# A fused attention and feed-forward kernel: a planned issue order, DMA transposes of q, k and x, and one score burst per block

## The chip, the cores and the metric

The kernel runs on one core of a Trainium2 chip. The metric is the device time of one execution in microseconds (us); lower is better. Executions carry a state, fast or slow.

PE is TensorE's matmuls and PEld its weight loads. DVE is VectorE, ACT is ScalarE, POOL is GpSimd. SP is the engine that issues most DMAs; "SPq" in a profile line is time in which SP's sequencer is occupied by issuing one.

## The reference

For each batch and head, scores are masked to a local window of 96 positions and 8 global positions, with a linear distance bias. The result of attention goes through a two-layer network with softplus:

```python
# q, k, v: (4, 8, 768, 64), float32; n_global 8, n_local 96
scores = q @ k.T / sqrt(64) - slope[h] * dist     # -1e9 where neither local nor global
a = softmax(scores)
x = (a @ v)                # regrouped as (3072 tokens, 512)
h = x @ w_in               # w_in (512, 2048)
g = softplus(h)            # log(1 + exp(h))
out = g @ w_out            # w_out (2048, 512), out (3072, 512) float32
```

## The kernel before

Tokens go in 24 blocks of 128; two blocks make a window of 256. Attention of later windows is interleaved with the two layers of earlier ones, by a hand-made list of event times. Within a window, partition p holds tokens 2p and 2p+1, so that a q or k load reads runs of 512 bytes.

q and k are cast to bf16, transposed by TensorE and copied out of PSUM; x is treated likewise. Scores are computed in two half bursts a block, four heads each, and DVE adds the bias.

```python
def load(w):
    nc.sync.dma_start(q32[:], q[b, :, sl, :].rearrange("h (p r) d -> p h (r d)", r=2))
    # k the same; v in four pieces of 256-byte runs
    ...
def transp(w, which, psum, eng):
    for r in range(2):
        for m in range(NPAIR):                  # 8 matmuls for a window of q or of k
            nc.tensor.transpose(tr[:, m, r, :], src[...], ident[:])
    cast_on[eng](t[:], psum...)                 # PSUM to SBUF
...
def scores(n, half, psum):
    for lh in range(4):
        nc.tensor.matmul(psum[:, reg_base(lh), :], kt_of(n)[rows, m, :], qT[rows, m, :])
        if i > 0:
            nc.tensor.matmul(psum[:, reg_base(lh) + 1, :], kt_of(n - 1)[rows, m, :], qT[rows, m, :])
    ...                                         # DVE: z = scores + bias
def mm2(g, p):                                  # second layer: two output banks
    for ns in range(2):
        for j in range(2):
            nc.tensor.matmul(o_ps[ns][:], gt[...], w_out_bf[...], ...)
```

The softmax here doesn't subtract the row's maximum and nothing guards it: scores larger than these inputs give would overflow.

Of the kernel before, what the change touches and what calls it, by code (L numbers as in the profile page):

```python
# [1 line left out]

# [8 lines left out]
ALU = mybir.AluOpType  # L11
F32 = mybir.dt.float32
BF16 = mybir.dt.bfloat16


@with_exitstack
def kernel(
# [33 lines left out]
    NGRP = NT // W  # L51
    NS = 4
    GH = NG // 2

    slopes = [2.0 ** (-8.0 * (h + 1) / H) for h in range(H)]

    root_d = float(D) ** 0.5
    perm = [0, 2, 1, 3]

    def reg_base(lh):  # L60
        return 4 * (lh % 2) + 2 * (lh // 2)

    ctx.enter_context(tc.manual_schedule())

    const = ctx.enter_context(tc.tile_pool(name="const", bufs=1))
    raw = ctx.enter_context(tc.tile_pool(name="raw", bufs=3))
    qkv = ctx.enter_context(tc.tile_pool(name="qkv", bufs=2))
    ring = ctx.enter_context(tc.tile_pool(name="ring", bufs=5))
    work = ctx.enter_context(tc.tile_pool(name="work", bufs=3))
    ffn = ctx.enter_context(tc.tile_pool(name="ffn", bufs=3))  # L70
    ps = ctx.enter_context(tc.tile_pool(name="ps", bufs=1, space=bass.MemoryType.PSUM))

    s_ps = ps.tile([P, 8, P], F32, name="s_ps")
    x_ps = ps.tile([P, 512], F32, name="x_ps")
    tr_ps = ps.tile([P, 1024], BF16, name="tr_ps")

# [9 lines left out]


    state = {}

    def load(w):  # L90
        b, ww = divmod(w, WPB)
        sl = slice(W * ww, W * ww + W)
        q32 = raw.tile([P, H, 2 * D], F32, tag="q32", name="q32")
        nc.sync.dma_start(q32[:], q[b, :, sl, :].rearrange("h (p r) d -> p h (r d)", r=2))
        k32 = raw.tile([P, H, 2 * D], F32, tag="k32", name="k32")
        nc.sync.dma_start(k32[:], k[b, :, sl, :].rearrange("h (p r) d -> p h (r d)", r=2))
        v32 = raw.tile([P, 2, H, D], F32, tag="v32", name="v32")
        for blk in range(2):
            t0 = W * ww + P * blk
            vv = v[b, :, t0 : t0 + P, :].rearrange("h (p r) d -> r p h d", r=2)  # L100
            for r in range(2):
                nc.sync.dma_start(v32[64 * r : 64 * r + 64, blk, :, :], vv[r])  # L102
        state["raw", w] = (q32, k32, v32)

    cast_on = {"pool": nc.gpsimd.tensor_copy, "dve": nc.vector.tensor_copy, "act": nc.scalar.copy}

    def cast(w, which, eng):
        q32, k32, v32 = state["raw", w]
        copy = cast_on[eng]
        if which in "qk":  # L110
            src = q32 if which == "q" else k32
            t = qkv.tile([P, 2, H, D], BF16, tag=which + "b", name=which + "b")
            copy(t[:], src[:].rearrange("p h (r d) -> p r h d", r=2))  # L113
            state[which + "b", w] = t
        else:
            t = ring.tile([P, 2, H, D + 1], BF16, tag="vb", name="vb")
            copy(t[:, :, :, 0:D], v32[:])
            nc.gpsimd.memset(t[:, :, :, D : D + 1], 1.0)
            state["vb", w] = t

    def transp(w, which, psum, eng):
        src = state[which + "b", w]
        tr = psum.rearrange("p (m r t) -> p m r t", m=NPAIR, r=2)
        for r in range(2):
            for m in range(NPAIR):
                nc.tensor.transpose(  # L126
                    tr[:, m, r, :],
                    src[:, r, 2 * m : 2 * m + 2, :].rearrange("p a b -> p (a b)"),
                    ident[:],
                )  # L130
        t = (ring if which == "k" else qkv).tile(
            [P, 2, NPAIR * 2, 64], BF16, tag=which + "T", name=which + "T"
        )
        cast_on[eng](t[:], psum.rearrange("p (a b t) -> p b a t", b=2, t=64))  # L134
        state[which + "T", w] = t

    def kt_of(n):
        return state["kT", n // 2][:, n % 2, :, :].rearrange("p (m r) t -> p m (r t)", r=2)

    def vb_of(n):  # L140
        return state["vb", n // 2][:, n % 2, :, :]

    def globals_k(n):


        first = n - n % NBLK
        kd = state["kT", (n - 1) // 2][:, (n - 1) % 2, :, 0:GH]
        nc.gpsimd.tensor_copy(kd, state["kT", first // 2][:, 0, :, 0:GH])  # L148

    def globals_v(n):  # L150
        first = n - n % NBLK
        for r in range(2):
            sl = slice(64 * r, 64 * r + GH)
            nc.vector.tensor_copy(vb_of(n - 1)[sl, :, 0:D], vb_of(first)[sl, :, 0:D])  # L154

    def scores(n, half, psum):
        i = n % NBLK
        qT = state["qT", n // 2][:, n % 2, :, :].rearrange("p (m r) t -> p m (r t)", r=2)
        for lh in range(4):
            h = 4 * half + lh  # L160
            m, sub = h // 2, h % 2
            rows = slice(64 * sub, 64 * sub + 64)
            nc.tensor.matmul(psum[:, reg_base(lh), :], kt_of(n)[rows, m, :], qT[rows, m, :])  # L163
            if i > 0:
                nc.tensor.matmul(  # L165
                    psum[:, reg_base(lh) + 1, :], kt_of(n - 1)[rows, m, :], qT[rows, m, :]
                )
        z = work.tile([P, 8, P], F32, tag="z", name="z")
        if i == 0:
            nc.vector.tensor_tensor(z[:, 0:4, :], psum[:, 0:8:2, :], bias0[:, half, :, :], ALU.add)  # L170
        else:
            nc.vector.tensor_tensor(z[:], psum[:, :, :], biasA[:, half, :, :], ALU.add)  # L172
        state["z", n, half] = z

    def expo(n, half):
        nr = 4 if n % NBLK == 0 else 8
        z = state.pop(("z", n, half))
        pb = work.tile([P, 8, P], BF16, tag="pb", name="pb")
        nc.scalar.activation(pb[:, 0:nr, :], z[:, 0:nr, :], AF.Exp, scale=1.0 / root_d)  # L179
        state["pb", n, half] = pb  # L180

    def pv(n, half, psum):
        i = n % NBLK
        pb = state.pop(("pb", n, half))
        if half == 0:
            state["xs", n] = work.tile([P, H, D], BF16, tag="xs", name="xs")
        xs = state["xs", n]
        xv = psum[:, 0 : 4 * (D + 1)].rearrange("p (h e) -> p h e", e=D + 1)
        for lh in range(4):
            h = 4 * half + lh  # L190
            j = perm.index(lh)
            if i == 0:
                nc.tensor.matmul(xv[:, lh, :], pb[:, j, :], vb_of(n)[:, h, :])
            else:
                nc.tensor.matmul(  # L195
                    xv[:, lh, :], pb[:, 2 * j, :], vb_of(n)[:, h, :], start=True, stop=False
                )
                nc.tensor.matmul(  # L198
                    xv[:, lh, :], pb[:, 2 * j + 1, :], vb_of(n - 1)[:, h, :], start=False, stop=True
                )  # L200
        rcp = work.tile([P, 4], F32, tag="rcp", name="rcp")
        nc.vector.reciprocal(rcp[:], xv[:, :, D : D + 1].rearrange("p h e -> p (h e)"))  # L202
        nc.vector.tensor_tensor(  # L203
            xs[:, 4 * half : 4 * half + 4, :],
            xv[:, :, 0:D],
            rcp[:][:, :, None].to_broadcast([P, 4, D]),
            ALU.mult,
        )

    def x_transp(n, psum, eng):  # L210
        xs = state.pop(("xs", n))
        tr = psum[:, 0:512].rearrange("p (m t) -> p m t", m=NPAIR)
        for m in range(NPAIR):
            nc.tensor.transpose(  # L214
                tr[:, m, :], xs[:, 2 * m : 2 * m + 2, :].rearrange("p a b -> p (a b)"), ident[:]
            )
        cast_on[eng](XT[:, :, P * n : P * n + P], tr)  # L217

    def mm1(g, p):
        hv = h_ps[state["hslot"]][:].rearrange("p (j t) -> p j t", j=2)  # L220
        state["hslot"] ^= 1
        for j in range(2):
            fb = 2 * p + j
            for m in range(NM):
                nc.tensor.matmul(  # L225
                    hv[:, j, :],
                    w_in_bf[:, m, fb * P : fb * P + P],
                    XT[:, m, W * g : W * g + W],
                    start=(m == 0),
                    stop=(m == NM - 1),  # L230
                )
        if p % 2 == 0:
            state["e", g] = ffn.tile([P, 2, 512], F32, tag="e", name="e")
        if p == 0:
            state["g", g] = ffn.tile([P, NFB, W], BF16, tag="g", name="g")
        e = state["e", g]
        nc.scalar.activation(e[:, p % 2, :].rearrange("p (j t) -> p j t", j=2), hv, AF.Exp)  # L237
        if p % 2 == 1:
# [4 lines left out]
                bias=1.0,  # L243
            )

    def mm2(g, p):
        gt = state["g", g]
        for ns in range(2):
            for j in range(2):
# [216 lines left out]
```

## Time and profile before

| | before |
|---|---|
| time, median of 2 runs | 259.94 us |
| span of the profiled run | 256.0 us |
| PE busy | 225.1 us, 88% |
| first-layer matmuls started by 52 us | 51 of 768 |
| second-layer matmuls started by 52 us | 12 of 384 |

The first lines to read are those of the page that cut the span into 40 slices. Each digit is the busy share of a slice in tenths; the DMA row is the mean busy share of the core's 16 DMA engines.

```profile
span 256.0 us, 5170 instructions
...
PE   1437687399999999999999999999999999999991
...
DMA  7999999999965095192291590300202003003033
```

PE is starved for the first eight slices while DMA is full; then PE is full to the end. The table by stretches says it in microseconds (columns: stretch, length, busy time and count of PE, PEld, DVE, ACT and POOL, granted PE clock, DMA share, GB/s; the DMA share adds up the times of packets, which can overlap, so it can pass 1):

```profile
0.00:52.00 52.00, 27.28 (x247) 18.76 (x248) 26.62 (x63) 21.78 (x26) 15.04 (x29) 0.94 1.17 224
52.00:88.00 36.00, 35.66 (x367) 25.36 (x366) 22.04 (x42) 26.59 (x37) 6.65 (x11) 0.99 0.76 160
88.00:196.00 108.00, 108.00 (x1090) 75.43 (x1089) 68.78 (x134) 74.85 (x98) 12.79 (x25) 1.00 0.40 89
```

PE is busy for all of 88 to 196. Its waits after 52 us (what waited, on whom; us in total, times, longest) are next to nothing:

```profile
PE o_ps_349 L251 <- DVE osb L260: 0.4, 1, 0.4
PE o_ps_349 L251 <- ACT g L239: 0.3, 1, 0.3
```

The start is bound by DMA. The chain of waits there (start, us, what) is a v load that takes 17 us while five windows and the weights share the queues:

```profile
28.38 2.02 SPq L102
...
30.44 17.32 DMA v_338<-in_v_dram
```

What one group of matmuls costs is read from starts, not from durations, because matmuls overlap. From PE's timeline, in a stretch where it never waits:

```profile
126.33 0.61 PE L126 MATMUL tr_ps<-ident,qb 128*128 128x128 bf16 x8
126.78 0.29 PE L193 MATMUL x_ps<-vb,pb 128*128 128x65 bf16 x4
```

The eight transposes of q occupy PE for 126.78 - 126.33 = 0.45 us, 0.056 us each. Read in this way, a window cost PE about 17.9 us.

### The profile page before, as it was taken

Reading aid. Unit: us, or ns where it says so; the run is one execution under the profiler, and the core shown is the slowest. Engines: PE = TensorE matmul, PEld = TensorE weight load, DVE = VectorE, ACT = ScalarE, POOL = GpSimd, SP = SyncE. Lnnn points to the kernel's source line nnn. Section 1 sums busy time; section 2 is a strip of 40 time slices with the busy share of each in tenths; the row PEclk is TensorE's granted clock in tenths of the full one; section 3 lists DMA queues with packets and bytes.
Section 4 is the critical chain, followed back from the end, with each engine's and each line's share of the span. In section 5 each row is a group of like instructions: output and inputs, shape, how many; then the busy total and the mean of one; then the engine's idle time right before and its main releaser. Section 6 shows DMA issues by size and latency. Waiting matters only on the chain.

```text
span 256.0 us, 5170 instructions
## 1 busy us (share of the span) xinstructions
PE 225.1 (88%) x2144; PEld 154.6 (60%) x2144; DVE 139.1 (54%) x279; ACT 156.2 (61%) x201; POOL 34.9 (14%) x66
## 2 busy tenths in 40 slices
PE   1437687399999999999999999999999999999991
PEld 1324465177667677666776766676676667666640
DVE  6475832246674865764665757746656757430012
ACT  2455544087876767767665777766577677766600
POOL 2142810130300300303001103030000000000000
PEclk9999999689999999999999999999999999999998
DMA  7999999999965095192291590300202003003033
GB/s 188 250 250 199 257 197 199 245 233 240 178 177 105 5 244 86 41 242 48 64 240 30 127 203 0 85 0 22 63 3 65 20 1 86 0 3 82 0 82 82
DMA packets 58391, 29.69 MB, mean 116 GB/s; under 512 B 26624, under 2 KB 55296, under 8 KB 58368
## 3 DMA queue, kind: packets, MB, share of 16 engines
q1 hardware_dynamic: 54144, 25.17, 45.5%
q0 software_dynamic: 4224, 4.19, 9.7%
q8 instruction: 16, 0.26, 0.5%
q14 instruction: 7, 0.06, 0.1%
HBM read 27.26 MB, written 6.29 MB: 131 GB/s over the span
## 4 chain that ended last, share of the span: by engine, by line
PE 79%; DMA 9%; ACT 3%; SPq 3%; DVE 3%; issue 1%; DVEq 0%; POOL 0%; POOLq 0%
PE o_ps_349 L251 17%; PE h_ps_348 L225 16%; PE o_ps_350 L251 16%; PE h_ps_347 L225 15%; DMA v_338<-in_v_dram 7%; PE s_ps L163 4%; PE tr_ps L126 3%; SPq L102 2%; DMA k_84<-in_k_dram 2%; PE tr_ps L214 2%; PE s_ps L165 2%; PE x_ps L195 2%; PE x_ps L198 2%; DVE z L172 1%; ACT g L239 1%
## 5 line engine op out<-in xcount | busy, mean ns | idle before, releaser
L225 PEld LDWEIGHTS <-w_in_bf 128*128 128x128 bf16 x768 | 73.2, 99 | 22.0 <-DVE XT L217 0.7
L172 DVE TENSOR_TENSOR z<-s_ps,biasA 128x1024 f32<-128x1024 f32 x38 | 46.4, 1220 | 26.1 <-PE s_ps L165 26.0
L251 PE MATMUL o_ps_349<-w_out_bf,g 128*128 128x512 bf16 x192 | 57.7, 383 | 1.1 <-ACT g L239 0.7
L251 PE MATMUL o_ps_350<-w_out_bf,g 128*128 128x512 bf16 x192 | 57.6, 382 | 0.0
L179 ACT ACTIVATE pb<-z 128x1024 bf16<-128x1024 f32 (+1 forms) x48 | 46.8, 975 | 14.4 <-DVE z L172 13.2
L237 ACT ACTIVATE e<-h_ps_348 128x512 f32<-128x512 f32 x48 | 28.6, 596 | 40.8 <-PE h_ps_348 L225 40.8
L251 PEld LDWEIGHTS <-g 128*128 128x128 bf16 x384 | 35.1, 98 | 29.8 <-issue 1.7
L225 PE MATMUL h_ps_347<-XT,w_in_bf 128*128 128x256 bf16 x384 | 51.5, 279 | 0.5 <-DVE XT L217 0.5
L239 ACT ACTIVATE g<-e 128x1024 bf16<-128x1024 f32 x48 | 50.7, 1057 | 1.5
L225 PE MATMUL h_ps_348<-XT,w_in_bf 128*128 128x256 bf16 x384 | 50.8, 276 | 0.0
L237 ACT ACTIVATE e<-h_ps_347 128x512 f32<-128x512 f32 x48 | 28.3, 589 | 22.2 <-PE h_ps_347 L225 22.0
L260 DVE COPY osb<-o_ps_349 128x512 f32<-128x512 f32 x12 | 8.3, 692 | 24.1 <-PE o_ps_349 L251 23.6
L202 DVE RECIPROCAL rcp<-x_ps 128x4 f32<-128x4 f32 x46 | 8.1, 176 | 24.4 <-PE x_ps L198 24.4
L203 DVE TENSOR_TENSOR xs<-x_ps,rcp 128x256 bf16<-128x256 f32 x46 | 19.5, 425 | 1.6
L148 POOL COPY kT<-kT 128x32 bf16<-128x32 bf16 x16 | 3.4, 213 | 121.0 <-PE s_ps L165 116.4
L126 PE MATMUL tr_ps<-ident,qb 128*128 128x128 bf16 x96 | 8.6, 242 | 11.7 <-DVE qb L113 11.7
L163 PE MATMUL s_ps<-qT,kT 64*128 64x128 bf16 x180 | 16.2, 231 | 2.8 <-ACT kT L134 2.2
L165 PE MATMUL s_ps<-qT,kT 64*128 64x128 bf16 x152 | 13.8, 228 | 5.5 <-POOL kT L148 5.5
L195 PE MATMUL x_ps<-vb,pb 128*128 128x65 bf16 x156 | 15.5, 198 | 1.3 <-DVE xs L203 1.3
L163 PEld LDWEIGHTS <-kT 64*128 64x128 bf16 x192 | 8.6, 99 | 12.3 <-issue 8.2
L198 PE MATMUL x_ps<-vb,pb 128*128 128x65 bf16 x156 | 15.4, 198 | 0.6 <-DVE vb L154 0.6
L134 DVE COPY qT<-tr_ps 128x1024 bf16<-128x1024 bf16 x11 | 7.6, 692 | 13.3 <-PE tr_ps L126 13.2
(86 smaller groups left out, 181.0 us busy)
## 6 DMA issues: line engine op xcount, KB each, us to landing
out_dram<-osb SPq DMA_DIRECT2D x48, 128.0 KB, 2.4
w_in_bf<-in_moe_w_in_dram POOLq DMA_DIRECT2D x4, 512.0 KB, 11.9
w_out_bf<-in_moe_w_out_dram POOLq DMA_DIRECT2D x4, 512.0 KB, 14.6
q_82<-in_q_dram SPq DMA_DIRECT2D x1, 512.0 KB, 4.2
k_84<-in_k_dram SPq DMA_DIRECT2D x1, 512.0 KB, 6.1
v_86<-in_v_dram SPq DMA_DIRECT2D x4, 128.0 KB, 5.0
q_91<-in_q_dram SPq DMA_DIRECT2D x1, 512.0 KB, 5.5
k_93<-in_k_dram SPq DMA_DIRECT2D x1, 512.0 KB, 7.0
```

The costliest lines, as they stand in the source:

```text
L126: nc.tensor.transpose(tr[:, m, r, :], src[:, r, 2 * m : 2 * m + 2, :].rearrange("p a b -> p (a b)"), ident[:],)
L163: nc.tensor.matmul(psum[:, reg_base(lh), :], kt_of(n)[rows, m, :], qT[rows, m, :])
L165: nc.tensor.matmul(psum[:, reg_base(lh) + 1, :], kt_of(n - 1)[rows, m, :], qT[rows, m, :])
L172: nc.vector.tensor_tensor(z[:], psum[:, :, :], biasA[:, half, :, :], ALU.add)
L179: nc.scalar.activation(pb[:, 0:nr, :], z[:, 0:nr, :], AF.Exp, scale=1.0 / root_d)
L195: nc.tensor.matmul(xv[:, lh, :], pb[:, 2 * j, :], vb_of(n)[:, h, :], start=True, stop=False)
L198: nc.tensor.matmul(xv[:, lh, :], pb[:, 2 * j + 1, :], vb_of(n - 1)[:, h, :], start=False, stop=True)
L203: nc.vector.tensor_tensor(xs[:, 4 * half : 4 * half + 4, :], xv[:, :, 0:D], rcp[:][:, :, None].to_broadcast([P, 4, D]), ALU.mult,)
L225: nc.tensor.matmul(hv[:, j, :], w_in_bf[:, m, fb * P : fb * P + P], XT[:, m, W * g : W * g + W], start=(m == 0), stop=(m == NM - 1),)
L237: nc.scalar.activation(e[:, p % 2, :].rearrange("p (j t) -> p j t", j=2), hv, AF.Exp)
L239: nc.scalar.activation(state["g", g][:, 2 * p - 2 : 2 * p + 2, :].rearrange("p a t -> p (a t)"), e[:].rearrange("p a t -> p (a t)"), AF.Ln ...
L251: nc.tensor.matmul(o_ps[ns][:], gt[:, fb, ns * P : ns * P + P], w_out_bf[:, fb, :], start=(fb == 0), stop=(fb == NFB - 1),)
```

## The change

The intent is to take transposes off the full engine and to fill the start. A small planner now simulates the engines with assumed durations and emits each engine's instructions in the simulated order. q and k from window 3 on, and x from block 4 on, are transposed by DMAs issued from SP. A block's 16 score matmuls are one burst over four PSUM banks; for that, one output bank and the bank of the transposes are given up. In the first four blocks TensorE adds a bf16 bias by a matmul with the identity. v is loaded in 512-byte runs, and the early loads and weights have an order of their own.

The diff is long; this is its core, with cuts marked.

```diff
+class Planner:      # list scheduling by rank over assumed durations; engines and DMA queues
+    LAT = {"PE": 0.30, "DVE": 0.12, "ACT": 0.12, "POOL": 0.15, "SP": 0.0}
 ...
-    for r in range(2):
-        for m in range(NPAIR):
-            nc.tensor.transpose(tr[:, m, r, :], ...)
+    if key is None:                       # q, k of windows 3 to 11
+        def fn():
+            for r in range(2):
+                for blk in range(2):
+                    last = nc.sync.dma_start_transpose(
+                        dst[:, blk, :, 64 * r : 64 * r + 64],
+                        src[64 * blk : 64 * blk + 64, r, :, :].rearrange("p h d -> p (h d)"))
+            return last
+        op(f"tr{which}{w}", "SP", 1.2, rank, fn, ..., dma=(1.6, 40.0))
 ...
+    # x of blocks 4 to 23
+    nc.sync.dma_start_transpose(XT[:, :, cols], xs[:].rearrange("p h d -> p (h d)"))
+    op(f"xt{n}", "SP", 0.42, rank, fn, ..., dma=(0.8, 40.0))
 ...
+    for m in range(NPAIR):                # one burst a block, row groups alternate
+        for u in range(u_all):
+            for part in range(2):
+                rows = slice(64 * part, 64 * part + 64)
+                nc.tensor.matmul(s_ps[:, reg, :], kt_of(n - u)[rows, m, :], qTt[rows, m, :], ...)
 ...
+    if biased:                            # blocks 0 to 3
+        nc.tensor.matmul(bank(key), ident[:], src[:, 512 * j : 512 * j + 512], start=True, stop=False)
 ...
-    o_ps = [late.tile([P, 512], F32, name=f"o_ps{i}") for i in range(2)]
+    o_ps = ps.tile([P, 512], F32, name="o_ps")
```

The numbers after "SP" are durations that the planner assumes: 1.2 us for the four transposes of a q or k window and 0.42 us for one of x.

## The prediction

> **What bounds the kernel now.** TensorE from 52 us on. The page gives PE 225.1 us busy of a 256.0 us span; the table by stretches shows PE busy 36.00 of 36.00 us in each stretch from 88 to 196, and PE's waits after 52 us sum to 0.7 us. Before 52 us it is starved (27 us busy, DMA share about 1.0 and over). There the chain of waits runs through one v load (17.3 us) and its issue (6.4 us), because five windows and all weights share the queues; only 54 of 768 first-layer matmuls are done by 52 us. The tail after the last matmul is 5.8 us.
>
> **One window (256 tokens) on PE**, from issue pitches in the timeline at 115 to 135 us: first layer 8 x 0.87 us and second layer 32 x 0.217, together 13.9; q and k transposes 16 x 0.056 = 0.9; x transposes 2 x 0.23 = 0.46; scores four half bursts of 0.33 plus 0.1 of gap, 1.7; probabilities times v 4 x 0.24 = 0.96. Sum 17.9, which matches the chain's repeat of 9.0 us per block.
>
> **What the change does.** It takes q and k transposes off PE from window 3, x transposes from block 4, and halves the number of score bursts (estimate from the pitch: 0.68 us a burst, so 0.3 saved a window). Together 1.65 us a window, 15 us over nine windows. It adds 14 bias matmuls of 0.22 us (3 us). PE's pure work, estimated: FFN 166.6, scores 15.6, values 10.6, remaining transposes 4, bias 3: 200 us (before 211).
> The start changes more: v comes in 512-byte runs instead of 256, w_in slices are queued early, three windows ahead of them. I expect first-layer matmuls from 16 us and, by 45 to 50 us, that layer of two to three groups done. PE's lost time at the start falls from about 35 us (52 less 17 of useful issue) to 13. DVE (139 us) and ACT (156 us) don't bound, but ACT will be near 75% busy.
>
> **Sum**: 200 + 13 lost at the start + 5.5 tail + 5 of new PE stalls (one output bank instead of two; orders planned with assumed durations) = 223.5 span; the time lies 3.9 above the span now, so **227 us**, range 219 to 239. Faster by over 2%: 0.95; within 2%: 0.03; slower: 0.02.
>
> **The open point** is the DMA transpose, in no trace yet. The Trainium skill, "VectorE: DVE Perf Modes", The three transpose paths, lists 1309 ns for a 128x128 tile by DMA; 24 tiles a window in series would be 31 us, above the 16.2 us window. "DMA: Bandwidth & Descriptors", Latency and other measured facts, gives 261 GB/s, by which I estimate 3 us for 0.79 MB. I side with the second: 16 engines share it, and attention runs over a window ahead.
>
> **Signs.** Right: PE over 90% busy from 30 us on; about 224 fewer transposes on PE; first-layer matmuls before 20 us; SP's queue busy below 70% of a window; ten DMA transposes a window landing in under 6 us. Wrong: PE waiting for kT, qT or XT from DMA once per window; over 1 us of SP issue per transpose; PE waiting over 0.5 us for each output copy.
>
> **What would break it**: transposes that fill SP's queue or hold the loads behind them; a late DMA under a fixed order, stalling PE in every window; weights landing after 55 us.

## The result, and the profile after

The changed kernel took 276.36 us (two runs, 275.71 and 277.01) against 259.94 us. The ratio is 1.065, 95% interval 1.056 to 1.073: slower. Ratios here and below are the mean time of one kernel's fast runs over that of the other's in the same rounds, so they are not quite the ratio of the medians quoted.

```profile
span 275.2 us, 4814 instructions
...
PE   2759777949249977598789968959974999999973
...
DMA  4899999593244656628767556648267372200111
```

PE now has holes everywhere. By stretches:

```profile
0.00:52.00 52.00, 37.14 (x347) 26.15 (x351) 24.19 (x69) 27.52 (x35) 21.89 (x44) 1.00 1.02 206
52.00:88.00 36.00, 23.17 (x219) 13.91 (x220) 17.23 (x33) 10.74 (x14) 7.60 (x15) 0.86 0.49 119
88.00:196.00 108.00, 91.21 (x825) 62.79 (x836) 49.93 (x90) 70.60 (x91) 23.36 (x42) 0.94 0.61 142
```

The start did improve: by 52 us, 128 first-layer matmuls have been started, against 51. The gain is lost at once: 13 us of the next 36 are idle, and 17 of the 108 after that. Idle PE also loses clock, 0.86 and 0.94 instead of 0.99 and 1.00. The Trainium skill ("TensorE: Matmul & The Clock Gate", Part 1) describes this as a gate that slows the array after idle stretches; the trace agrees: PE's longest wait, 8.6 us, ends at 79.3 us, and from 75.8 to 82.6 us the granted clock is 0.50. The clock shown for the first 52 us says less: the trace has no record of it before 24.6 us and counts it as full, though the first transposes start 107 ns apart, twice the 56 ns read above.

PE's waits, longest first in total:

```profile
PE x_ps L535 <- DVE xs L548: 9.0, 3, 3.8
PE h_ps L593 <- DMA XT<-xs: 8.6, 1, 8.6
PE s_ps L485 <- DMA kT<-kb: 8.3, 5, 3.2
PE o_ps L635 <- DVE osb L652: 6.4, 5, 2.2
PE s_ps L467 <- DVE bias L723: 5.2, 1, 5.2
```

They name different tiles, so the list alone gives no cause. SP's queue does. Its instructions in part of a window (start, us occupied, what, count):

```profile
89.42 0.39 SPq L293 DMA_DIRECT2D k<-in_k_dram  x1
89.90 1.87 SPq L578 DMA_TRANSPOSE XT<-xs  x1
91.90 5.47 SPq L369 DMA_TRANSPOSE qT<-qb  x4
97.48 0.52 SPq L293 DMA_DIRECT2D v<-in_v_dram  x1
98.10 1.21 SPq L578 DMA_TRANSPOSE XT<-xs  x1
99.41 5.07 SPq L369 DMA_TRANSPOSE kT<-kb  x4
104.57 0.53 SPq L293 DMA_DIRECT2D q<-in_q_dram  x1
```

A plain load occupies SP for about 0.5 us, a transpose for 1.2. The view by tile gives minimum, median and maximum in ns over all of them:

```profile
L369 SPq DMA_TRANSPOSE qT<-qb x36: 1171/1240/2665, 45.8 to 216.1; - x36
L578 SPq DMA_TRANSPOSE XT<-xs x20: 1189/1210/2516, 62.9 to 235.6; - x20
```

Eight of 1.24 and two of 1.21 are 12.3 us a window; three loads of about 0.5 and two stores of about 0.5 bring it to about 15 us, nearly all of the 16.2 us that I had counted for a window on PE. Between 88 and 196 us SP is occupied for 82 us of 108, 70 of them by transposes (each instruction's own time in the trace, summed). It is not quite full, but it works in order, so a load whose buffer is free still stands behind transposes, and a transpose waits for its cast. The chain of waits shows both:

```profile
99.41 1.19 SPq L369
100.65 1.24 SPq L369
101.94 2.38 DMA kT<-kb
105.81 7.14 DMA k<-in_k_dram
114.94 1.07 PE h_ps L593 x5
```

The k transposes are issued one by one, the scores of the window's first block wait for the third of the four (the last that they need) to land, and the next k load leaves at 105.81, behind all four. DVE's order is fixed too, so its cast of that k stands before the work that would free PE:

```profile
113.04 0.69 DVE L320 CAST kb<-k 128x1024 bf16<-128x1024 f32 x1 [1.70 <-DMA v<-in_v_dram]
113.65 0.18 DVE L547 RECIPROCAL rcp<-x_ps 128x4 f32<-128x4 f32 x1
113.86 0.42 DVE L548 TENSOR_TENSOR xs<-x_ps,rcp 128x256 bf16<-128x256 f32 x1
```

PE continues at 114.34, right after the last of these. That is how a late load reads as "PE waits for DVE xs".

### The profile page after: what moved, and what is told of

The parts are those of the page before. It is cut to its first block, busy times and chain, and to the rows that moved or that the text cites. A ratio compares the mean times of both kernels' runs of the same rounds, so it can differ in the third digit from the quotient of the medians.

```text
span 275.2 us, 4814 instructions
## 1 busy us (share of the span) xinstructions
PE 218.3 (79%) x1905; PEld 146.2 (53%) x1934; DVE 113.1 (41%) x227; ACT 152.4 (55%) x193; POOL 62.0 (23%) x117
## 4 chain that ended last, share of the span: by engine, by line
PE 46%; DMA 22%; SPq 14%; DVE 9%; issue 5%; ACT 2%; DVEq 0%
PE o_ps L635 20%; PE h_ps L593 18%; DMA q<-in_q_dram 11%; SPq L369 9%; DMA kT<-kb 6%; DMA k<-in_k_dram 4%; PE s_ps L485 3%; SPq L298 3%; DVE z L510 3%; DVE osb L652 2%; DVE xs L548 2%; PE x_ps L535 1%; PE x_ps L538 1%; SPq L578 1%; ACT e L609 1%
## 5 line engine op out<-in xcount | busy, mean ns | idle before, releaser
L593 PE MATMUL h_ps<-XT,w_in_bf 128*128 128x256 bf16 x768 | 101.6, 283 | 10.7 <-DMA XT<-xs 8.6
L635 PE MATMUL o_ps<-w_out_bf,g 128*128 128x512 bf16 x357 | 95.6, 393 | 8.5 <-DVE osb L652 6.4
L593 PEld LDWEIGHTS <-w_in_bf 128*128 128x128 bf16 x768 | 75.8, 101 | 33.3 <-DMA XT<-xs 9.1
L609 ACT ACTIVATE e<-h_ps 128x512 f32<-128x512 f32 x96 | 59.3, 626 | 56.4 <-PE h_ps L593 55.9
L519 ACT ACTIVATE pb<-z 128x1024 bf16<-128x1024 f32 (+1 forms) x40 | 39.3, 987 | 42.1 <-DVE z L510 41.7
L652 DVE COPY osb<-o_ps 128x512 f32<-128x512 f32 x24 | 16.5, 688 | 57.2 <-PE o_ps L635 57.2
L339 POOL CAST vb<-v 64x512 bf16<-64x512 f32 x44 | 27.4, 622 | 52.8 <-DMA v<-in_v_dram 51.1
L446 POOL COPY vb<-vb 4x512 bf16<-4x512 bf16 x32 | 19.6, 613 | 59.4 <-PE x_ps L538 58.5
L485 PE MATMUL s_ps<-qT,kT 64*128 64x128 bf16 x352 | 15.7, 233 | 12.2 <-DMA kT<-kb 8.3
L535 PE MATMUL x_ps<-vb,pb 128*128 128x65 bf16 x160 | 16.3, 201 | 10.8 <-DVE xs L548 9.0
L538 PEld LDWEIGHTS <-pb 128*128 128x128 bf16 x160 | 12.3, 103 | 11.5 <-issue 9.4
L320 DVE CAST qb<-q 128x1024 bf16<-128x1024 f32 x11 | 7.6, 692 | 24.2 <-DMA q<-in_q_dram 22.6
L535 PEld LDWEIGHTS <-pb 128*128 128x128 bf16 x160 | 13.6, 103 | 5.7 <-ACT pb L519 3.1
L538 PE MATMUL x_ps<-vb,pb 128*128 128x65 bf16 x160 | 16.3, 201 | 0.0
```

The lines of the kernel that those rows point to most:

```text
L339: copy_on[eng](dst[64 * r : 64 * r + 64, :, 0:D], src[64 * blk : 64 * blk + 64, :, D * r : D * r + D],)
L485: nc.tensor.matmul(s_ps[:, reg, :], kt_of(n - u)[rows, m, :], qTt[rows, m, :], start=not biased, stop=True, skip_group_check=biased,)
L519: nc.scalar.activation(pb[:, 0:nr, :], src, AF.Exp, scale=1.0 / root_d)
L535: nc.tensor.matmul(xv[:, m, :], pb[:, 2 * m, :], vb[n % NVB][:, h, :], start=True, stop=False)
L538: nc.tensor.matmul(xv[:, m, :], pb[:, 2 * m + 1, :], vb[(n - 1) % NVB][:, h, :], start=False, stop=True,)
L593: last = nc.tensor.matmul(hv[:, j, :], w_in_bf[:, m, fb * P : fb * P + P], XT[:, m, W * g : W * g + W], start=(m == 0), stop=(m == NM - 1),)
```

## The experiments

Theory A: each DMA transpose instruction occupies SP for 1.2 us whatever its size, and this stalls PE through late loads and late transposes. Rival B: the transposes' data slows the other DMAs. Rival C: the planned order, the single output bank, or other parts of the change do the harm. Each variant is compared with the kernel before in the same rounds (three); all gave correct results. The medians are over all runs of a variant, slow ones too; the ratios use fast runs alone, so they decide.

| run | median us | ratio to before | 95% interval |
|---|---|---|---|
| all transposes on PE | 254.59 | 0.971 | 0.964 to 0.979 |
| plan told the true durations | 262.58 | 1.011 | 1.005 to 1.016 |
| loads issued by POOL | 263.26 | 1.010 | 1.002 to 1.017 |
| true durations and loads by POOL | 258.41 | 0.993 | 0.987 to 0.999 |
| q, k on PE; x by DMA | 243.45 | 0.933 | 0.926 to 0.940 |
| x on PE; q, k by DMA | 265.45 | none | (one fast run, 260.50) |
| q, k transposes merged | 235.84 | 0.907 | 0.904 to 0.910 |
| merged, plan told the old durations | 238.07 | 0.912 | 0.906 to 0.919 |
| merged, small extra transposes | 264.52 | 1.017 | 1.013 to 1.020 |
| merged, x on PE | 242.40 | 0.931 | 0.926 to 0.936 |
| merged, x in pairs | 234.57 | 0.902 | 0.894 to 0.909 |
| merged, without bias matmuls | 236.89 | 0.911 | 0.908 to 0.915 |
| merged, score rows not alternating | 238.81 | 0.920 | 0.915 to 0.925 |
| merged, window 2 off the output bank | 238.26 | 0.913 | 0.907 to 0.919 |
| merged, window 3 loads later | 238.19 | 0.915 | 0.911 to 0.920 |

### All transposes back on TensorE

```diff
-        transp("q", w, tr_key.get(("q", w)), ...)
+        transp("q", w, tr_key.get(("q", w), ("x",)), ...)     # k and x the same
```

> All transposes of q, k and x back on TensorE (through the bank of the value products), every other part of the change kept. Theory A (each DMA transpose takes 1.2 us of the SP queue's issue time, ten a window, and loads queue in order behind them) and rival B (transposes slow the data path of the other DMAs) both expect PE to be full again after the start: its work grows by about 11 us to 211, so 232 us of span, 236 us of time, plus or minus 6. Rival C (the planned order, the single output bank and the other parts stall PE whatever does the transposes) expects 262 us or more.

It took 254.59 us (fast runs 251.24 and 254.07). Against 276 this clears rival C of most of the loss: the planner and everything else of the change are still there, and the kernel beats the one before. But it missed my 236 by far. Two terms of my sum were off. PE's largest wait is the copy of the single output bank, 6.4 us in 12 waits. And the start loses more than I thought (see the last comparison).

### The plan told the true durations

```diff
-op(f"tr{which}{w}", "SP", 1.2, ...)     op(f"xt{n}", "SP", 0.42, ...)
+op(f"tr{which}{w}", "SP", 5.05, ...)    op(f"xt{n}", "SP", 1.25, ...)
```

> The same instructions as the changed kernel; only the durations by which the planner orders them are corrected to the measured ones (5.05 us of SP for the four transposes of a q or k window instead of 1.2, 1.25 for one of x instead of 0.42). If the wrong durations in the plan are the whole cause, 232 to 245 us, with SP still at 15 us a window. If SP's capacity is the cause (15 us needed of a 16.2 us window, in order, with waits between), the gain is small: 258 us or more. Rival B expects no change beyond 2%.

262.58 us: 14 us better than 276, but 27 us from what the same planner reaches with fewer transposes (below). The wrong durations are a part of the loss, not the whole. SP was occupied for 95.5 us of 108 in the stretch from 88 to 196, nearly all of the time.

### Fewer, larger transposes

The DVE cast of q and k writes its columns in the order (head pair, token parity, head, d). Then one transpose covers a block's both parities: two of 64 x 1024 replace four of 64 x 512, with the same bytes and the same destination layout.

```diff
-for r in range(2):
-    for blk in range(2):
-        nc.sync.dma_start_transpose(dst[:, blk, :, 64 * r : 64 * r + 64], src[64 * blk : 64 * blk + 64, r, :, :]...)
+for blk in range(2):
+    nc.sync.dma_start_transpose(dst[:, blk, :, :].rearrange("p m (r t) -> p (m r) t", r=2),
+                                src[64 * blk : 64 * blk + 64, :, :, :].rearrange("p a h d -> p (a h d)"))
```

> Two DMA transposes of 64 x 1024 for a q or k window instead of four of 64 x 512; the cast writes the columns in the order that makes this possible; the planner is told 2.5 and 1.25 us. Same bytes. Theory A with a cost per instruction (64 x 512 and 128 x 512 both took 1.2 us): 1.2 us each again, SP down from 15 to 10 us a window, time 232 to 247. If the issue cost grows with the bytes, each takes 2.4 us and the time stays at 262 us or more; rival B expects that too.

235.84 us, ratio 0.907: it beats the kernel before by 9%. SP's part of a window in this variant, from SP's timeline:

```profile
123.81 2.52 SPq L373 DMA_TRANSPOSE qT<-qb  x2
126.43 0.52 SPq L293 DMA_DIRECT2D v<-in_v_dram  x1
127.04 1.22 SPq L582 DMA_TRANSPOSE XT<-xs  x1
128.78 2.51 SPq L373 DMA_TRANSPOSE kT<-kb  x2
```

The view by tile for q's transposes of the same variant (minimum, median and maximum in ns):

```profile
L373 SPq DMA_TRANSPOSE qT<-qb x18: 1200/1262/2607, 45.6 to 174.5; - x18
```

Twice the bytes in an instruction, and the median goes from 1240 to 1262 ns. PE is full again:

```profile
52.00:88.00 36.00, 33.61 (x332) 22.18 (x335) 22.78 (x43) 21.86 (x29) 10.24 (x19) 1.00 0.73 175
88.00:196.00 108.00, 106.26 (x1030) 73.60 (x1046) 61.66 (x107) 83.99 (x109) 30.66 (x55) 1.00 0.77 168
```

Rival B falls here. The same bytes move in less time (DMA share 0.77 against 0.61), and the median time from issue to landing of a q or k transpose even grew, from 2.4 us to 2.7 and 3.6; the kernel is 40 us faster all the same.

### Loads of q, k, v moved to another queue

```diff
-return nc.sync.dma_start(dst[:], src[b, :, sl, :]...)
+return (nc.gpsimd if w >= 3 else nc.sync).dma_start(dst[:], src[b, :, sl, :]...)
```

> The loads of q, k, v from window 3 on are issued by GpSimd instead of SP, so they no longer stand behind the transposes; transposes unchanged. Theory A, in its form that the late loads do the harm: SP falls by about 1.5 us a window only, but the load to cast wait of DVE (28 us in the profile for q and k) shrinks below 12 us and the time to 240 to 258. If the transposes alone fill SP too late, DVE's waits shrink but the time stays above 262. Rival B expects no change.

263.26 us: about 13 us better than the changed kernel, less than the form "late loads alone" expected, and more than rival B did (no change). Its waits are not used.

### True durations and loads on the other queue

> The changed kernel with the corrected plan (262.6 us) and, besides, the loads of q, k, v from window 3 on issued by GpSimd. If SP's capacity for the transposes is what binds (about 12.4 us of transposes and 1 us of stores a window, nothing else left on it), 252 to 260 us: the gain of about 1.5 us of SP a window. If late loads behind the transposes are what binds, 245 us or less. No change within 2 us would say that the way from transpose to scores binds and the loads never did.

258.41 us, in the range for capacity. With the durations told, moving the loads is worth 1.8% in all (0.993 against 1.011). This doesn't measure what loads behind transposes cost, because the move also hurt the start: the k load of window 2 took 22.7 us to land, at 53.4 (16.0 us and 45.4 with all loads on SP), and the second layer began at 56.5 us, not 48.1. From 88 to 196 us, PE was busy for 100.5 us, against 94.1 with the loads on SP and 106.3 in the merged variant above. There, about half of the shortfall went with the loads. So both the loads behind the transposes and the transposes' own occupation of SP count; their shares are not settled.

### The count of instructions put back

After each merged transpose stands a small one of 64 x 128 into a scratch tile of its own, which nobody reads.

```diff
+    nc.sync.dma_start_transpose(next(toll)[:], src[64 * blk : 64 * blk + 64, 0, 0:2, :]...)
-op(f"tr{which}{w}", "SP", 2.5, ...)
+op(f"tr{which}{w}", "SP", 5.05, ...)
```

> The merged variant with a small extra DMA transpose (64 x 128, a quarter of the old piece, into a scratch tile that nobody reads) after each of the real ones of q and k: the instruction count of the changed kernel is back, bytes only 1/8 more for q and k, and the planner is told 5.05 us as in the variant with the corrected plan (262.6 us). If SP's cost is per instruction, the extra ones take about 1.2 us each and the time goes back to 255 to 268 us. If it is per byte, they take 0.3 us and the time stays below 242.

```profile
L378 SPq DMA_TRANSPOSE toll<-qb x18: 1212/1226/2098, 48.1 to 208.7; - x18
L374 SPq DMA_TRANSPOSE qT<-qb x18: 1215/1266/3217, 45.4 to 207.4; - x18
```

264.52 us, beside the 262.58 us of the unmerged kernel with the same durations told. A transpose of 16 KB occupies SP for 1.23 us, one of 128 KB for 1.27. The cost is per instruction, and putting the count back puts the loss back. Nor is it that the scores wait for more transposes in a row: here a window's first block needs only the first of the four of k, in the changed kernel the third. Beside the merged variant this run changes two things, the count and what the plan is told (5.05 against 2.5), and no run told the merged variant 5.05. With the plan held fixed, the next run shows the same. The two together settle that the count is the cause.

### Merged, but the plan told the old durations

> The merged variant (four DMA transposes a window for q and k instead of eight), but the planner is told the old, wrong 1.2 us for a q or k window and 0.42 us for x. Separates fewer instructions from a better plan. If the number of instructions is what matters, 236 to 244 us; if the plan's knowledge is needed too, 245 to 255; if it was the plan alone, over 258.

238.07 us, against 276.36 us for the changed kernel with the same durations told. The two differ in the count and in the column order of the cast, which takes 0.69 us in both. With the count of q and k halved, what the plan knows of SP is worth about 2 us, if anything (the intervals overlap). With the old count it was worth 14.

### q and k on PE alone, or x on PE alone

> From the changed kernel, q and k of all windows are transposed by TensorE, only x (two transposes a window) by DMA. Theory A (cost per DMA transpose instruction on SP: 1.2 us each, so 2.4 us a window here) expects no stall from SP: the all-TensorE variant's 254.6 us less the x transposes (20 blocks of 0.23 us, 4.6 us), 247 to 253 us. A theory in which the x transposes, not those of q and k, do the harm expects 265 or more.

> From the changed kernel, only x goes back to TensorE; q and k keep their eight DMA transposes a window (10 us of SP a window, with the plan still told 2.4). Theory A expects most of the loss to stay: 262 to 275 us. If x did the harm, 250 or less.

Two DMA transposes a window: 243.45 us, a gain over all on PE. Eight a window: 265.45 us, three of its four runs slow and the fast one at 260.50. Both fit theory A, no stall at two and most of the loss at eight; the first came out better than I expected, and the one fast run of the second lies just below its range. The size of the second isn't explained: by the sum above SP would be occupied for about 12.4 us of 16.2 there, and yet it takes over 20 us more than six transposes a window in the run before, with equally wrong durations. About 6 to 7 of these are x on PE (next run); what makes the rest of the step from six to eight so dear stays open.

### x back on PE in the merged variant

> The merged variant with x back on TensorE (20 blocks of 0.23 us on PE, 2.4 us a window less on SP). If x by DMA is worth its PE time only, 235.8 + 4.6 = 238 to 242 us. The pair without DMA for q and k showed 11 us for it (254.6 against 243.5), so if the single bank that x then shares with the value products costs more than PE time, 243 to 248 us.

242.40 us, between the two expected ranges: x by DMA is worth 6 to 7 us here (0.931 against 0.907), and about 10 between the two unmerged variants (0.971 against 0.933). PE's own time for 20 blocks of x is 4.6 us. That the rest is the shared bank of the value products was only argued, not shown.

### Merged, and x in pairs

> The merged variant with one x transpose of 128 x 1024 a window instead of two of 128 x 512 (x laid out by block, four x buffers instead of three). SP falls from about 10 to 8.8 us a window. If SP still limits the merged variant, 2 to 6 us faster, 230 to 234 us; if it doesn't any more, within 1.5 us of 235.8.

234.57 us, with an interval that overlaps the merged variant's (they ran in different rounds). No gain is shown, so nothing says that SP still limits.

### Four checks of the other parts, on the merged variant

```diff
-PE_BIAS = 4                                          # without bias matmuls
+PE_BIAS = 0
-for m ...: for u ...: for part in range(2):          # rows not alternating
+for part in range(2): for m ...: for u ...:
-("q", 2): ("o",), ("k", 2): ("o",)                   # window 2 off the output bank
+("q", 2): ("x",), ("k", 2): ("x",)
-gates[which, w] = [marks[w - 3, ...]]                # window 3 loads later
+gates[which, w] = [loads["out", 2]] if w == 3 else [marks[w - 3, ...]]
```

> The merged variant without the bias matmuls: DVE adds the bias in the first four blocks too. 14 matmuls of 0.22 to 0.5 us leave PE (it starts with a 5.2 us wait for the bias), DVE gets 8 additions of 0.7 to 1.2 us. In the start PE isn't the limit (it waits for data), so: within 3 us of 235.8, I expect 236 to 238.

> The merged variant; the 16 matmuls of a score burst are issued 8 on the lower 64 rows, then 8 on the upper, instead of alternating. If alternating lets two row groups work at once, a burst grows from 0.62 us (issue of 16 in 0.55) to over 0.9 us, 24 bursts, so the time grows by about 7 us to 241 to 245; if not, it stays within 1 us.

> The merged variant; the transposes of window 2's q and k go through the bank of the value products instead of the output bank, in which they made the first second-layer matmuls wait (first one at 48.4 us although its weights had landed before, because the plan keeps the order of uses of a bank). If that order is a cost of the start, second-layer matmuls start before 40 us and the time falls by 3 to 6 us to 230 to 233; if the DMA alone limits the start, no change within 1 us.

> The merged variant; window 3's loads wait for the third w_out slice to land instead of for first-layer matmuls of window 0, so that they no longer compete with window 2 and the weights. In the merged run k of window 2 took 16 us to land, at 45.7. If this competition holds the start up, k of window 2 lands by 40 us and the time falls by 3 to 6 us to 230 to 233; if the start is limited by the sum of bytes or by later windows coming late, no gain or a loss.

Without the bias matmuls: 236.89 us, no difference shown. The start waits for data, so neither PE's 14 matmuls nor DVE's eight additions count.

A burst of 16 score matmuls in PE's timeline of the merged variant:

```profile
120.09 0.62 PE L489 MATMUL s_ps<-qT,kT 64*128 64x128 bf16 x16
```

And with the rows not alternating, where it lengthens from 0.62 to 0.86 us:

```profile
120.03 0.86 PE L489 MATMUL s_ps<-qT,kT 64*128 64x128 bf16 x16
```

The time rose by about 3 us (0.920 against 0.907), half of what I expected. So alternating row groups does let two 64-row matmuls overlap. The Trainium skill ("TensorEngine Tiling (Array Packing)", Key Properties) says that different tiles can run matmuls in parallel; the trace agrees: in the alternating burst they start in pairs 3 to 4 ns apart, a pair every 56 ns or so, in the other one mostly one by one, 56 ns apart.

Window 2 off the output bank: second-layer matmuls began at 36.8 us instead of 48.4 (a profile of the slow state), yet the time did not fall. Window 3 loads later: the cast of k of window 2 began at 43.5 us instead of 45.7, and the time rose by about 2 us. Neither gave the 3 to 6 us hoped for; that both only moved a wait in the start is argued, not shown. Between 52 and 88 us PE in the second of these was busy for 31.45 us where the merged variant had 33.61. What a better start would take stays open.

## Why the prediction was wrong, point by point

- **The step that failed: the DMA transposes.** The prediction named the risk and then sided with bandwidth, "16 engines share it", and with a lead, "attention runs over a window ahead". After the start the bytes were not the limit, and the lead did not hold. The term missing from the sum was SP's issue time, 10 instructions of 1.2 us a window. It surfaced in the term "5 of new PE stalls": from 52 us to its last matmul, PE of the changed kernel was idle for 37.9 us, in the merged variant for 5.9. The runs put the price of the count at about 38 us, both with the old durations in the plan: 276.36 us with eight a window for q and k, 238.07 with four. Telling the plan the truth without lowering the count returns about 14 us.
- **The start was mis-sized.** I put PE's lost time at 13 us. In the merged variant, where little is lost later, it is about 24: PE's work of 200 us (my estimate), plus 24, a tail of 4 and about 6 of waits after 52 us give its span of 234.2, so the 24 is what is left over, no better than the 200. "Two to three groups" of the first layer by 45 to 50 us were two (128 of 768 matmuls, by 52 us); the first-layer work began at 21.1 us in the changed kernel, 5 us later than forecast and after the 20 us of the sign.
- **The steady mechanism was right in size where SP is not in the way.** In the merged variant it can be read from counts: from 88 to 196 us, 428 first-layer and 209 second-layer weight loads at 0.109 and 0.217 us make 92.0 of 108 us. A window of 13.9 us of network work then takes 13.9 x 108 / 92.0 = 16.3 us; the prediction said 16.2.
- **The output bank** costs about what was guessed for all new stalls in the all-TensorE variant (6.4 us of waits against 5), and 2.4 us in the merged one.
- **The bias matmuls** did no visible harm, as predicted.
- **Signs.** "Over 1 us of SP issue per transpose" was listed as a sign of being wrong, and it is the one that came true, with "PE waiting for kT, qT or XT from DMA", though in six waits and not in every window (kT 8.3 us in five, XT 8.6 us in one). SP's queue, forecast below 70% of a window, was occupied for 76% (82 us of 108). The sign "ten transposes landing in under 6 us" came true and meant nothing: landing took medians of 2.4 to 4.2 us. Issue, not landing, was the cost.

## What to carry to other kernels

Before moving work to DMAs, count instructions on the issuing queue, not only bytes: multiply the issue time of one by their number in a period, and compare with the period. If the cost is per instruction, change the layout upstream (here the order in which a cast writes its columns; the cast took 0.69 us before and after) so that one instruction covers more. A planner that fixes the order of all engines turns one wrong duration into waits on engines that have nothing to do with it, so check its durations against a trace first.

## What the Trainium skill lacked or had wrong

- "DMA: Bandwidth & Descriptors" (Latency and other measured facts) gives the transpose a bandwidth, 261 GB/s; the page's rules for kernel authors advise the hardware DMA transpose. What decided here, how long one transpose holds the issuing queue on this chip, it lacks (it has only sequencer cycles of "previous generations", in a table on trn3 B0, with no time by size): on SP, one SBUF to SBUF transpose occupied the queue for 1.23 us at 64 x 128, 1.24 at 64 x 512, 1.21 at 128 x 512 and 1.26 at 64 x 1024 (medians), while a plain load of 512 KB took 0.4 to 0.5 (medians of the changed kernel; up to 5.2 in its crowded start).
- The same page (Issuing engines are not separate DMA queues) calls the sequencer's time to initiate a DMA "usually small relative to the DMA itself". For these transposes it was half of the 2.4 us from issue to landing, and it does not overlap with the next issue on the same queue.
- "VectorE: DVE Perf Modes" (The three transpose paths) lists 1309 ns for a 128 x 128 tile by DMA, without saying how it goes with size: 128 x 512, four such tiles, was issued in 1.21 us and landed in a median of 4.2 us (2.5 in the run with the count put back), and 64 x 512 in a median of 2.4 us. Four times the listed time would be 5.2 us, an estimate from that page's figure.
- No page that I looked up says how a planned order should leave room for a late DMA; the old durations cost 14 us with eight transposes a window for q and k, and about 2 with four.
